# Sketched attention and four dense branches: a rearranged end, one more block in three products, and working tiles that begin at multiples of 64 bytes

## The chip, the cores and the metric

The kernel runs on one core of one Trainium2 chip, in one launch. The metric is the device time of that core in microseconds (us), the median of several executions. A separate execution was recorded by the hardware profiler; all the profile lines come from that one.

## The reference

Polynomial-sketch attention feeds a sum of four two-layer branches, weighted by token. In short:

```python
# q, k, v: (4 batches, 4 heads, 1088 tokens, 32); S1, S2: (8, 32)
a, b = x @ S1.T, x @ S2.T                      # x is q or k
phi(x) = outer(a, b)                           # 64 features a token and head
kv, z = phi(k).T @ v, phi(k).sum(tokens)
attn = (phi(q) @ kv) / (phi(q) @ z + 1e-6)
x = attn, heads side by side                   # (4352 tokens, 128)
p = domain_probs / (domain_probs.sum(-1) + 1e-9)
out = sum over e of p[:, e] * (relu(x @ w1[e]) @ w2[e])   # w1: 128 x 1024, w2: 1024 x 128, e = 0..3
```

Everything is float32.

## The kernel before

**Chunks, units, steps.** The 4352 tokens are cut into chunks `CHUNKS`: 128, 448, seven of 480, and 416 (numbers m = 0 to 9). A chunk passes through the four branches e = 0 to 3 one after the other; a pair (m, e) is called a unit here. The hidden layer has 1024 features, that is eight blocks k = 0 to 7 of 128. A step is two blocks, so a unit is four steps or eight half-steps, and a chunk is `NQ` = 16 steps; step 16m + 4e opens unit (m, e). Features lie on the 128 partitions and tokens along the free axis.

**First layer.** From chunk 1 on, the product of tokens and first weights is made of three faster products (type `F32R`): the tokens are split into `xa`, `xb`, `xd` and the weights into `wa`, `wb`, `wd`. `first` issues `wa`·`xa` and `wb`·`xb`, ScalarE scales the sum in PSUM (L1144), and one half-step later `third` adds `wd`·`xd` (L1194).

**Second layer.** For most blocks the hidden values are split too: ScalarE makes `ha` (L1198), VectorE makes `hb` (L1170, in `lower`) and, for two blocks at a time, `hd` (L1173). The three products with `vab`, `vb`, `vd` are called a, b and d. Any other block is one plain float32 product, called x, of `hid` (L1208, a ReLU on ScalarE) and the unsplit weights `w_sb`. Which blocks of a unit take three products is told by three sets: six blocks by default, seven for units in `MORE_IN`, all eight for units in `ALL_IN`. The split weights of the seventh and eighth blocks are made by `more_weight_parts` at steps listed by hand, in tiles called `vm` that reuse the room of attention tiles (`fs`, `y`, `sr`, `kvz` and others).

**The order on TensorE** is written by hand. `DEAL`, `DEAL_MORE`, `DEAL_ALL` and `DEAL_END` give each product of a unit a half-step, counted from the unit's first, at which it becomes due (`to_due`, `behind`, `passed`); within a half-step they go in the order of the list. Products a and b add up in PSUM tile o0, d and x in tile o1. When the last a or b is issued, ScalarE evacuates o0 (L1277). When the last d or x is issued, `gather` adds o1, multiplies by the token's weight `gate` and adds to `total` (for most units on GpSimd, L1357 to L1366), and it loads the gates of a later unit from DRAM (`load_gates`, SyncE's queue).

**The end.** The last unit is (9, 3), with `DEAL_END`. Its block 7 is left for the end as an x (`x7`): VectorE takes the ReLU and multiplies by `gate` in one operation (L1204). `finish` adds o1 to the evacuated o0, multiplies by `gate` and adds `total`, in three slices: tokens 256 to 415 (multiply and add on GpSimd), 0 to 127, 128 to 255. `by_token` first multiplies x7's hidden values by the weights with tokens on the output's partitions (L1300), then adds the finished sum through a product with the identity `eye` (L1306), which turns it to the same form. Copies bring the result from PSUM to `rows` (L1311), and four DMAs store it (L1314), two from SyncE's queue and two from ScalarE's.

**Where tiles lie.** The pools are laid one after the other, and each tile takes a multiple of 32 bytes of a partition. Up to `dsum` the sizes add up so that the next tile, `x_first`, begins 32 bytes past a multiple of 64. So do the tiles behind it in the pool `const` (`ring`, which holds the tokens, `wa`, `wb`, `wd`, and the four `vb`), and all tiles of the pools `loads` and `attn` but one. `rc`, the last one of `attn`, takes 96 bytes for its 20 numbers, and the pool `moe` behind it (`xa`, `xb`, `xd`, `ha`, `hb`, `hd`, `hid`, `gate`, `ev`, `total`) begins at a multiple of 64. Of the weights, `vab`, `vd` and `w_sb` lie ahead of `dsum`, at multiples of 64.

Of the kernel before, what the change touches and what calls it, by code (L numbers as in the profile page):

```python
# [25 lines left out]
def kernel(  # L26
# [24 lines left out]
    nc = tc.nc  # L51

    P = 128
    HP = 64
    B, H, S, D = q.shape
    E, DM, F = w1.shape
# [8 lines left out]
    XW = 640  # L65
# [10 lines left out]
        a0=4, b0=4, a1=4, b1=4, a3=5, x2=5, d0=6, d1=6, a4=7, b3=7, a5=8, b4=8, b5=9, d3=9, d4=9,  # L76
# [4 lines left out]
        a0=4, b0=4, a1=4, b1=5, a2=5, a3=5, d0=6, d1=6, b2=6, a4=7, b3=7, a5=8, b4=8, d2=8, d3=8,  # L81
# [5 lines left out]
        b5=9, a6=9, a7=9, b6=10, b7=10, d4=10, d5=11, d6=11, d7=12,  # L87
    )
    DEAL_END = dict(
        a0=4, b0=4, a1=4, b1=5, a2=5, a3=5, d0=6, d1=6, b2=6, a4=7, b3=7, a5=8, b4=8, d2=9, d3=9,  # L90
        b5=9, x6=10, d4=10, d5=10, x7=11,
    )
    ALL_IN = {(7, 1), (7, 2), (8, 1), (8, 2), (9, 1), (9, 2)}
    UNITS = [[P, 448, 512], [576, 512], [576, 512], [576, 512]]

    SPLITS = [
# [280 lines left out]
    def parts(m):  # L377

        c, end, at = START[m], START[m] + CHUNKS[m], 0
        while c < end:  # L380
            n = min(end, (c // S + 1) * S) - c
            yield c // S, c % S, n, at
            c, at = c + n, at + n

    gate = {}

    def load_gates(m, experts, queue=nc.sync):
        for e in experts:
            gate[m, e] = mpool.tile([P, CW], F32, tag="gate", bufs=2, name="gate")
            for b, c, n, at in parts(m):  # L390
                queue.dma_start(gate[m, e][:, at : at + n], gates[b, e, c : c + n].partition_broadcast(P))

# [280 lines left out]
    def attend_inverse(nd, laid):  # L673

        tiles, banks = banks_of(laid)
        rc = apool.tile([P, XW // 32], F32, tag="rc", name="rc")
        for i, t0, t1 in banks:
            nc.vector.tensor_scalar(
                out=rc[:, H * t0 : H * t1],
                in0=_ap(nd[i], 0, P, D, [[D + 1, H * (t1 - t0)]]),  # L680
                scalar1=1e-6, scalar2=1.0, op0=ALU.add, op1=ALU.mult,
            )
        nc.vector.reciprocal(rc[:, 0 : H * tiles], rc[:, 0 : H * tiles])
        return rc
# [261 lines left out]
    def more_weight_parts(e, k=OTHER[0]):  # L946

        w = second_weight(e, k)
        if k != OTHER[0]:
            abd = apool.tile([P, 3 * P], F32R, tag="fs" if e == 2 else "y", name="vm")  # L950
            a, b, d = (abd[:, P * i : P * i + P] for i in range(3))
        elif e % 2 == 0:
            if "sr" not in more_home:
                more_home["sr"] = cpool.tile([P, 6 * P], F32R, tag="sr", name="vm")
            a, b, d = (more_home["sr"][:, P * i : P * i + P] for i in range(3 * (e // 2), 3 * (e // 2) + 3))
        else:
            ab = apool.tile([P, 2 * P], F32R, tag="kvz", bufs=2, name="vm")
# [231 lines left out]
    def third():  # L1189

        while begun:
            i, j, k, g, w, x = begun.pop(0)
            n = g.shape[-1]
            nc.tensor.matmul(g, w, x, start=False, stop=True, skip_group_check=True)  # L1194
            m, e = steps[i][0], steps[i][1] // NP
            if k in three_of(m, e) and not whole(m, e):
                (ha, hb, hc), both_of = three_tiles(k, n, three_of(m, e))
                nc.scalar.activation(ha, g, ACTF.Relu, scale=NEAR)  # L1198
# [60 lines left out]
    def passed(m, e, what, k, hd):  # L1259

        n, o = CHUNKS[m], 0 if what in "ab" else 1
        if what == "x" and at_end(m, e) and k == FB - 1:
            return by_token(m, e, k, hd)
        if (m, e) not in acc:
            acc[m, e] = [None, None]
        if acc[m, e][o] is None:
            acc[m, e][o] = psum(ps_o, f"o{o}")
        first_one = (m, e, o) not in begun_o
        begun_o.add((m, e, o))
        last = last_of(m, e, o) == what + str(k)  # L1270
        b = block_of(m, e, k)
        w, h = (second_weight(e, b), hd) if what == "x" else (w2_parts[e][b]["abd".index(what)], hd["abd".index(what)])
        nc.tensor.matmul(acc[m, e][o][:, 0:n], w, h, start=first_one, stop=last)  # L1273
        if last and o == 0:
            tag = "rest" if at_end(m, e) else "ev"
            evs[m, e] = mpool.tile([P, CW], F32, tag=tag, bufs=1, name=tag)
            nc.scalar.activation(evs[m, e][:, 0:n], acc[m, e][0][:, 0:n], ACTF.Copy, scale=1.0 + R12)  # L1277
        if last and o == 1:
            finish(m, e) if at_end(m, e) else close(m, e)

    def finish(m, e):

        n, o1, ev, g = CHUNKS[m], acc.pop((m, e))[1], evs.pop((m, e)), gate.pop((m, e))
        for x, eng in ((slice(2 * P, n), nc.gpsimd), (slice(0, P), nc.vector), (slice(P, 2 * P), nc.vector)):
            nc.vector.tensor_tensor(out=ev[:, x], in0=ev[:, x], in1=o1[:, x], op=ALU.add)
            eng.tensor_tensor(out=ev[:, x], in0=ev[:, x], in1=g[:, x], op=ALU.mult)
            eng.tensor_tensor(out=ev[:, x], in0=ev[:, x], in1=total[m][:, x], op=ALU.add)
        last_sum[0] = ev

    last_sum = [None]  # L1290
# [1 line left out]
    def by_token(m, e, k, hd):  # L1292

        n = CHUNKS[m]
        ((b, at, _, _),) = parts(m)
        rows = lpool.tile([P, 4 * P], F32, tag="kn", name="rows")
        y = [psum(ps_h, "h") for _ in range(3)]
        cols = [(c, min(P, n - c), y[min(c // P, 2)], max(c - 2 * P, 0)) for c in range(0, n, P)]
        for c, w, to, x in cols:
            nc.tensor.matmul(  # L1300
                to[0:w, x : x + P], hd[:, c : c + w], second_weight(e, block_of(m, e, k)),
                start=(x == 0), stop=False, skip_group_check=True,
            )
        for part, copy in ((cols[0:1], nc.scalar.copy), (cols[2:], nc.scalar.copy), (cols[1:2], nc.vector.tensor_copy)):
            for c, w, to, x in part:
                nc.tensor.matmul(  # L1306
                    to[0:w, x : x + P], last_sum[0][:, c : c + w], eye[0][:, :],
                    start=False, stop=True, skip_group_check=True,
                )
            for c, w, to, x in part:  # L1310
                copy(rows[0:w, c : c + P], to[0:w, x : x + P])  # L1311
        for g in range(4):
            t = len([c for c in cols if c[1] > 32 * g])
            (nc.scalar if g % 2 else nc.sync).dma_start(  # L1314
                bass.AP(out.tensor, out.offset + (b * S + at // 32 + g) * DM, [[G * DM, 32], [4 * DM, t], [1, DM]]),
                _ap(rows, 32 * g, 32, 0, [[P, t], [1, DM]]),
            )
# [218 lines left out]
```

## Time and profile before

| what | value |
|---|---|
| median of 3 executions | 445.34 us (444.56 to 445.58) |
| the profiled execution | 445.73 us, span of the recorded instructions 443.8 us |
| TensorE busy | 436.2 us, 98% of the span |
| VectorE, ScalarE, GpSimd busy | 391.7, 345.7, 169.4 us |
| granted TensorE clock, mean | 0.995 of full speed |
| chain that ended last | TensorE 94%, VectorE 3%, DMA 1% |

The span runs from the first recorded instruction to the last; the time of the execution is 1.9 us more. A group's row gives its source line, engine, operation, output and inputs by tile name, shape and count, and then: busy us, mean ns of one | idle us of the engine just before them, with what ended that idle time. "PEld" is TensorE's weight load, which overlaps its products. A row of the timeline gives start and duration in us.

### The profile page before, as it was taken

How to read it: one execution, taken by the hardware profiler on the slowest of the kernel's cores; microseconds unless marked ns; L12 is line 12 of the kernel's file. 1: busy time of each engine (PE TensorE's matmuls, PEld its weight loads, DVE VectorE, ACT ScalarE, POOL GpSimd, SP SyncE). 2: the span in 40 equal slices, each digit the busy share in tenths (PEclk: the TensorE clock that was granted, in tenths of full speed). 3: DMA queues.
4: the chain of work that ended last, by engine and by line, in shares of the span. 5: the costliest groups of instructions: out<-in, count | busy, mean ns of one | idle time of the engine just before them, and what ended most of it. 6: DMA issues, size and time to landing. Idle time of an engine off the chain costs nothing.

```text
span 443.8 us, 8131 instructions
## 1 busy us (share of the span) xinstructions
PE 436.2 (98%) x2768; PEld 359.9 (81%) x2768; DVE 391.7 (88%) x623; ACT 345.7 (78%) x725; POOL 169.4 (38%) x244
## 2 busy tenths in 40 slices
PE   8999999999999999999999999999999999999994
PEld 5887678888887888878887888787888888889993
DVE  5998969978999889988998899989999998998994
ACT  4478888858878688868884888687888988888881
POOL 6348623212142023213351344132333673564372
PEclk9999999999999999999999999999999999999997
DMA  7956375225502331235104621251320112002100
GB/s 224 285 139 168 84 172 117 76 51 123 154 24 45 112 102 24 73 78 149 24 23 61 152 25 44 46 147 38 69 46 22 23 33 57 2 24 44 36 20 21
DMA packets 45561, 35.02 MB, mean 79 GB/s; under 512 B 21744, under 2 KB 40304, under 8 KB 45520
## 3 DMA queue, kind: packets, MB, share of 16 engines
q1 hardware_dynamic: 43952, 33.28, 30.3%
q0 software_dynamic: 1184, 1.05, 1.0%
q8 instruction: 22, 0.36, 0.3%
q10 hardware_dynamic: 384, 0.17, 0.2%
q14 instruction: 19, 0.16, 0.1%
HBM read 29.27 MB, written 5.21 MB: 78 GB/s over the span
## 4 chain that ended last, share of the span: by engine, by line
PE 94%; DVE 3%; DMA 1%; issue 1%; ACT 0%; SPq 0%; DVEq 0%; ACTq 0%
PE o L1273 41%; PE h L1194 14%; PE h L1142 14%; PE h L1143 14%; PE h L273 6%; PE o L1252 3%; PE h L460 1%; DMA kn<-in_k_dram 1%; PE o L273 1%; DVE qp L588 1%; PE h L1306 0%; DVE qa L870 0%; DVE rd L620 0%; DVE kp L482 0%; DVE qf L860 0%
## 5 line engine op out<-in xcount | busy, mean ns | idle before, releaser
L1144 ACT ACTIVATE h<-h 128x480 f32<-128x480 f32 (+2 forms) x288 | 158.9, 552 | 63.4 <-PE h L1143 56.2
L1170 DVE SCALAR_TENSOR_TENSOR hb<-h,ha 128x480 fp32r<-128x480 f32 (+2 forms) x229 | 142.6, 638 | 22.2 <-ACT ha L1198 20.7
L1173 DVE SCALAR_TENSOR_TENSOR hd<-ha,hb 128x960 fp32r<-128x960 f32 (+3 forms) x121 | 140.6, 1162 | 11.7 <-DVE hb L1170 0.5
L1198 ACT ACTIVATE ha<-h 128x480 fp32r<-128x480 f32 (+2 forms) x229 | 128.6, 561 | 0.1
L1142 PE MATMUL h<-xa,wa 128*128 128x480 f32 (+2 forms) x288 | 128.0, 445 | 0.0
L1194 PE MATMUL h<-xd,wd 128*128 128x480 f32 (+2 forms) x288 | 108.7, 378 | 0.1
L1143 PE MATMUL h<-xb,wb 128*128 128x480 f32 (+2 forms) x288 | 108.1, 375 | 0.0
L1364 POOL TENSOR_TENSOR ev<-ev,gate 128x256 f32<-128x256 f32 (+3 forms) x52 | 46.3, 890 | 143.3 <-DVE ev L1351 135.7
L1273 PE MATMUL o<-ha,vab 128*128 128x480 f32 (+2 forms) x204 | 76.8, 377 | 0.0
L1142 PEld LDWEIGHTS h<-xa,wa 128*128 128x128 f32 x288 | 54.2, 188 | 17.2 <-issue 10.6
L1143 PEld LDWEIGHTS h<-xb,wb 128*128 128x128 f32 x288 | 54.2, 188 | 16.9 <-issue 10.9
L1273 PE MATMUL o<-hd,vd 128*128 128x480 f32 (+2 forms) x204 | 64.1, 380 | 0.0
L1194 PEld LDWEIGHTS h<-xd,wd 128*128 128x128 f32 x288 | 54.0, 188 | 9.2 <-ACT h L1144 0.8
L1366 POOL TENSOR_TENSOR total<-total,ev 128x256 f32<-128x256 f32 (+3 forms) x52 | 56.6, 1088 | 4.1
L1273 PE MATMUL o<-hb,vb 128*128 128x480 f32 (+2 forms) x136 | 51.2, 376 | 0.0
L1357 POOL TENSOR_TENSOR ev<-ev,rest 128x256 f32<-128x256 f32 (+2 forms) x24 | 19.4, 830 | 61.7 <-ACT rest L1354 61.7
L1273 PEld LDWEIGHTS o<-hd,vd 128*128 128x128 f32 x204 | 37.9, 188 | 6.1 <-issue 0.9
L1273 PEld LDWEIGHTS o<-ha,vab 128*128 128x128 f32 x204 | 38.3, 188 | 5.1
L1273 PE MATMUL o<-hid,w_sb 128*128 128x480 f32 (+2 forms) x84 | 40.2, 560 | 0.0
L1208 ACT ACTIVATE hid<-h 128x480 f32<-128x480 f32 (+2 forms) x58 | 32.5, 560 | 0.9 <-PE h L1194 0.8
L1364 POOL TENSOR_TENSOR total<-ev,gate 128x256 f32<-128x256 f32 (+3 forms) x18 | 15.7, 895 | 39.3 <-issue 23.9
L1273 PEld LDWEIGHTS o<-hb,vb 128*128 128x128 f32 x136 | 25.5, 188 | 4.0 <-DVE hb L1170 0.4
(167 smaller groups left out, 472.3 us busy)
## 6 DMA issues: line engine op xcount, KB each, us to landing
gate<-gates SPq DMA_DIRECT2D x16, 240.0 KB, 3.5
kn<-in_k_dram SPq DMA_DIRECT2D x4, 544.0 KB
vn<-in_v_dram SPq DMA_DIRECT2D x16, 128.0 KB, 6.7
qp<-qd SPq DMA_DIRECT2D x8, 256.0 KB
qp<-qd SPq DMA_DIRECT2D x6, 288.0 KB, 4.7
qb<-qd SPq DMA_DIRECT2D x6, 288.0 KB
qn<-in_q_dram SPq DMA_DIRECT2D x3, 544.0 KB
w_sb<-in_moe_w_dram SPq DMA_DIRECT2D x3, 512.0 KB
```

Source lines behind the costliest of these rows:

```text
L273: nc.tensor.matmul(out(s), weights(s), moving(s), **flags)
L1142: nc.tensor.matmul(g, wa[:, e, w], xa, start=True, stop=False)
L1143: nc.tensor.matmul(g, wb[:, e, w], xb, start=False, stop=True)
L1144: nc.scalar.activation(g, g, ACTF.Copy, scale=1.0 + R12)
L1170: nc.vector.scalar_tensor_tensor(out=hb, in0=g, scalar=0.0, in1=high, op0=ALU.max, op1=ALU.subtract)
L1173: nc.vector.scalar_tensor_tensor(out=d2, in0=a2.bitcast(F32), scalar=R12, in1=b2.bitcast(F32), op0=ALU.mult, op1=ALU.subtract)
L1194: nc.tensor.matmul(g, w, x, start=False, stop=True, skip_group_check=True)
L1198: nc.scalar.activation(ha, g, ACTF.Relu, scale=NEAR)
L1208: nc.scalar.activation(hid[i][j], g, ACTF.Relu)
L1273: nc.tensor.matmul(acc[m, e][o][:, 0:n], w, h, start=first_one, stop=last)
L1364: nc.gpsimd.tensor_tensor(out=to[:, x], in0=ev[:, x], in1=g[:, x], op=ALU.mult)
L1366: nc.gpsimd.tensor_tensor(out=total[m][:, x], in0=total[m][:, x], in1=ev[:, x], op=ALU.add)
```

## The change

- One number tile more in the pool `const`: `by_row`, 16 bytes a partition, laid between `dsum` and `x_first`. `rc` gets 8 numbers more. Because of these two, the tiles from `x_first` to `rc` move by 32 bytes and those of `moe` by 64: all the tiles named above as lying 32 bytes off now begin at multiples of 64 (the second buffer of `kvx`, the one exception above, goes the other way).
- `by_row` holds the gates of the last chunk's branch 3 with tokens on partitions (four numbers a partition). A DMA on SyncE's queue, right behind that unit's `gate`, fills it, number by number.
- Unit (8, 0) joins `ALL_IN`: its block 7 becomes three products. The weights for it are split at steps 119 and 121, in the room of the attention tile `qa`.
- `DEAL_END`: b5 moves ahead of d2 and d3 within the same half-step.
- At the end, x7's ReLU goes from VectorE to ScalarE, behind the evacuation of o0, without the gate. The gate is applied by ScalarE after x7's product, in PSUM, with one number a partition from `by_row`. The evacuated o0 of tokens 0 to 255 is multiplied by the gate, and `total` added to it, ahead of o1's end (`near_end`). `finish` multiplies o1 by the gate for tokens 0 to 255 in one piece and adds it; then come tokens 256 to 415, now all on VectorE. The first two groups of tokens share one PSUM tile and one copy.

```diff
     DEAL_END = dict(
-        a0=4, b0=4, a1=4, b1=5, a2=5, a3=5, d0=6, d1=6, b2=6, a4=7, b3=7, a5=8, b4=8, d2=9, d3=9,
-        b5=9, x6=10, d4=10, d5=10, x7=11,
+        a0=4, b0=4, a1=4, b1=5, a2=5, a3=5, d0=6, d1=6, b2=6, a4=7, b3=7, a5=8, b4=8, b5=9,
+        d2=9, d3=9, x6=10, d4=10, d5=10, x7=11,
     )
-    ALL_IN = {(7, 1), (7, 2), (8, 1), (8, 2), (9, 1), (9, 2)}
+    ALL_IN = {(7, 1), (7, 2), (8, 0), (8, 1), (8, 2), (9, 1), (9, 2)}
...
     gate = {}
+    by_row = cpool.tile([P, 4], F32, name="by_row")
...
                 queue.dma_start(gate[m, e][:, at : at + n], gates[b, e, c : c + n].partition_broadcast(P))
+            if (m, e) == (NC - 1, E - 1):
+                ((b, c, n, at),) = parts(m)
+                queue.dma_start(by_row[:, :], gates[b, e, c : c + 4 * P].rearrange("(i p) -> p i", p=P))
...
-        rc = apool.tile([P, XW // 32], F32, tag="rc", name="rc")
+        rc = apool.tile([P, XW // 32 + 8], F32, tag="rc", name="rc")
...
-            abd = apool.tile([P, 3 * P], F32R, tag="fs" if e == 2 else "y", name="vm")
+            abd = apool.tile([P, 3 * P], F32R, tag={0: "qa", 1: "y", 2: "fs"}[e], name="vm")
...
                 if at_end(m, e) and k == FB - 1:
-                    nc.vector.scalar_tensor_tensor(
-                        out=hid[i][j], in0=g, scalar=0.0, in1=gate[m, e][:, 0:n], op0=ALU.max, op1=ALU.mult
-                    )
+                    last_block.append((hid[i][j], g))
                     continue
...
             nc.scalar.activation(evs[m, e][:, 0:n], acc[m, e][0][:, 0:n], ACTF.Copy, scale=1.0 + R12)
+            if at_end(m, e):
+                near_end(m, e)
...
+    def near_end(m, e):
+        n, ev, g = CHUNKS[m], evs[m, e], gate[m, e]
+        ((h, of),) = last_block
+        nc.scalar.activation(h, of, ACTF.Relu)
+        x = slice(0, 2 * P)
+        nc.vector.tensor_tensor(out=ev[:, x], in0=ev[:, x], in1=g[:, x], op=ALU.mult)
+        nc.vector.tensor_tensor(out=ev[:, x], in0=ev[:, x], in1=total[m][:, x], op=ALU.add)
     def finish(m, e):
-        for x, eng in ((slice(2 * P, n), nc.gpsimd), (slice(0, P), nc.vector), (slice(P, 2 * P), nc.vector)):
-            nc.vector.tensor_tensor(out=ev[:, x], in0=ev[:, x], in1=o1[:, x], op=ALU.add)
-            eng.tensor_tensor(out=ev[:, x], in0=ev[:, x], in1=g[:, x], op=ALU.mult)
-            eng.tensor_tensor(out=ev[:, x], in0=ev[:, x], in1=total[m][:, x], op=ALU.add)
+        x = slice(0, 2 * P)
+        nc.vector.tensor_tensor(out=t[:, x], in0=o1[:, x], in1=g[:, x], op=ALU.mult)
+        nc.vector.tensor_tensor(out=ev[:, x], in0=ev[:, x], in1=t[:, x], op=ALU.add)
+        x = slice(2 * P, n)
+        nc.vector.tensor_tensor(out=ev[:, x], in0=ev[:, x], in1=o1[:, x], op=ALU.add)
+        nc.vector.tensor_tensor(out=ev[:, x], in0=ev[:, x], in1=g[:, x], op=ALU.mult)
+        nc.vector.tensor_tensor(out=ev[:, x], in0=ev[:, x], in1=t[:, x], op=ALU.add)
...
     def by_token(m, e, k, hd):
...
-        for part, copy in ((cols[0:1], nc.scalar.copy), (cols[2:], nc.scalar.copy), (cols[1:2], nc.vector.tensor_copy)):
-            for c, w, to, x in part:
-                nc.tensor.matmul(
-                    to[0:w, x : x + P], last_sum[0][:, c : c + w], eye[0][:, :],
...
-            for c, w, to, x in part:
-                copy(rows[0:w, c : c + P], to[0:w, x : x + P])
...
+        pair = y[0]
+        y = [y[0][:, 0:P], y[0][:, P : 2 * P], y[1][:, 0:P], y[2][:, 0:P]]
+        for i, c, w in cols:
+            nc.tensor.matmul(
+                y[i][0:w], hd[:, c : c + w], second_weight(e, block_of(m, e, k)),
+                start=i != 1, stop=True, skip_group_check=True,
+            )
+        for i, c, w in cols:
+            nc.scalar.activation(y[i][0:w], y[i][0:w], ACTF.Copy, scale=by_row[0:w, i : i + 1])
+        for i, c, w in cols:
+            nc.tensor.matmul(
+                y[i][0:w], last_sum[0][:, c : c + w], eye[0][:, :], start=False, stop=True, skip_group_check=True
+            )
+            if i == 1:
+                nc.vector.tensor_copy(rows[:, 0 : 2 * P], pair[:, 0 : 2 * P])
+            elif i:
+                (nc.vector.tensor_copy if i == 2 else nc.scalar.copy)(rows[0:w, c : c + P], y[i][0:w])
...
-    for e, at in ((2, (113, 117)), (1, (114, 115))):
+    for e, at in ((2, (113, 117)), (1, (114, 115)), (0, (119, 121))):
```

More of the change, by code (lines that the diff above doesn't have):

```diff
@@ L1277, in passed @@
             nc.scalar.activation(evs[m, e][:, 0:n], acc[m, e][0][:, 0:n], ACTF.Copy, scale=1.0 + R12)
+            if at_end(m, e):
+                near_end(m, e)
         if last and o == 1:
             finish(m, e) if at_end(m, e) else close(m, e)
-    def finish(m, e):
-        n, o1, ev, g = CHUNKS[m], acc.pop((m, e))[1], evs.pop((m, e)), gate.pop((m, e))
-        for x, eng in ((slice(2 * P, n), nc.gpsimd), (slice(0, P), nc.vector), (slice(P, 2 * P), nc.vector)):
-            nc.vector.tensor_tensor(out=ev[:, x], in0=ev[:, x], in1=o1[:, x], op=ALU.add)
-            eng.tensor_tensor(out=ev[:, x], in0=ev[:, x], in1=g[:, x], op=ALU.mult)
-            eng.tensor_tensor(out=ev[:, x], in0=ev[:, x], in1=total[m][:, x], op=ALU.add)
+    last_block = []
+    def near_end(m, e):
[5 more added lines that the diff above has]
+        nc.vector.tensor_tensor(out=ev[:, x], in0=ev[:, x], in1=total[m][:, x], op=ALU.add)
+    def finish(m, e):
+        n, o1, ev, g, t = CHUNKS[m], acc.pop((m, e))[1], evs.pop((m, e)), gate.pop((m, e)), total.pop(m)
+        x = slice(0, 2 * P)
[5 more added lines that the diff above has]
+        nc.vector.tensor_tensor(out=ev[:, x], in0=ev[:, x], in1=t[:, x], op=ALU.add)
         last_sum[0] = ev
@@ L1297, in by_token @@
         y = [psum(ps_h, "h") for _ in range(3)]
-        cols = [(c, min(P, n - c), y[min(c // P, 2)], max(c - 2 * P, 0)) for c in range(0, n, P)]
-        for c, w, to, x in cols:
+        pair = y[0]
+        y = [y[0][:, 0:P], y[0][:, P : 2 * P], y[1][:, 0:P], y[2][:, 0:P]]
+        cols = [(i, c, min(P, n - c)) for i, c in enumerate(range(0, n, P))]
+        for i, c, w in cols:
             nc.tensor.matmul(
-                to[0:w, x : x + P], hd[:, c : c + w], second_weight(e, block_of(m, e, k)),
-                start=(x == 0), stop=False, skip_group_check=True,
-            )
-        for part, copy in ((cols[0:1], nc.scalar.copy), (cols[2:], nc.scalar.copy), (cols[1:2], nc.vector.tensor_copy)):
-            for c, w, to, x in part:
-                nc.tensor.matmul(
-                    to[0:w, x : x + P], last_sum[0][:, c : c + w], eye[0][:, :],
-                    start=False, stop=True, skip_group_check=True,
-                )
-            for c, w, to, x in part:
-                copy(rows[0:w, c : c + P], to[0:w, x : x + P])
+                y[i][0:w], hd[:, c : c + w], second_weight(e, block_of(m, e, k)),
+                start=i != 1, stop=True, skip_group_check=True,
+            )
+        for i, c, w in cols:
[8 more added lines that the diff above has]
+                (nc.vector.tensor_copy if i == 2 else nc.scalar.copy)(rows[0:w, c : c + P], y[i][0:w])
         for g in range(4):
-            t = len([c for c in cols if c[1] > 32 * g])
+            t = len([w for _, _, w in cols if w > 32 * g])
             (nc.scalar if g % 2 else nc.sync).dma_start(
```

## The prediction

> **What bounds the kernel now.** I read the page's busy times and chain first, then the time by stretches (one for each unit of chunk 8), then the groups, and last the timeline of the end.
>
> ```profile
> PE 436.2 (98%) x2768; PEld 359.9 (81%) x2768; DVE 391.7 (88%) x623; ACT 345.7 (78%) x725; POOL 169.4 (38%) x244
> PE 94%; DVE 3%; DMA 1%; issue 1%; ACT 0%; SPq 0%; DVEq 0%; ACTq 0%
> ```
>
> TensorE (PE) sets the time from about 28 us to 435 us. In that stretch an edit is worth what it takes from TensorE, or what it adds there by making it wait. Outside lie the start (VectorE and loads) and the last 8 us.
>
> ```profile
> 353.66:364.29 10.63, 10.63 (x49) 8.83 (x47) 9.58 (x13) 9.16 (x19) 7.71 (x11) 1.00 0.12 26
> 364.29:374.90 10.61, 10.61 (x48) 8.83 (x47) 9.20 (x13) 9.14 (x19) 5.36 (x6) 1.00 0.26 46
> 374.90:385.38 10.48, 10.48 (x49) 9.02 (x48) 9.81 (x13) 9.06 (x19) 2.98 (x3) 1.00 0.06 23
> ```
>
> These are units (8, 0), (8, 1), (8, 2), each from its first product to the next unit's: length, then busy us of PE, PEld, DVE, ACT, POOL. TensorE has no gap; VectorE (DVE) has about 1 us left in each. A unit's last products fall due in the next unit, so the plain float32 product x7 of (8, 0) runs in the second row, which is the longer for it.
>
> ```profile
> L1142 PEld LDWEIGHTS h<-xa,wa 128*128 128x128 f32 x288 | 54.2, 188 | 17.2 <-issue 10.6 <-PE h L460 0.2 <-DVE qT L575 0.2
> L1273 PEld LDWEIGHTS o<-ha,vab 128*128 128x128 f32 x204 | 38.3, 188 | 5.1
> L1273 PEld LDWEIGHTS o<-hb,vb 128*128 128x128 f32 x136 | 25.5, 188 | 4.0 <-DVE hb L1170 0.4
> L1170 DVE SCALAR_TENSOR_TENSOR hb<-h,ha 128x480 fp32r<-128x480 f32 x188 | 119.2, 648 | 17.2 <-ACT ha L1198 15.9 <-PE h L1143 0.9
> L898 DVE SCALAR_TENSOR_TENSOR xb<-xa,ring 128x480 fp32r<-128x480 f32 x7 | 4.5, 649 | 0.0
> ```
>
> `wa`, `vb` and `ring` lie 32 bytes off a multiple of 64; `vab`, `h`, `ha` do not. The rows make no difference between them.
>
> ```profile
> 433.41 1.34 POOL L1366 TENSOR_TENSOR total<-total,ev 128x160 f32<-128x160 f32 x1
> 433.89 0.35 PE L1273 MATMUL o<-hb,vb 128*128 128x416 f32 x1
> 434.28 0.52 ACT L1277 ACTIVATE rest<-o 128x416 f32<-128x416 f32 x1 [0.78 <-PE o L1273]
> ...
> 435.16 1.16 PE L1300 MATMUL h<-w_sb,hid 128*128 128x128 f32 x8
> 435.43 0.52 DVE L1285 TENSOR_TENSOR rest<-rest,o 128x160 f32<-128x160 f32 x2 [0.56 <-PE o L1273]
> 435.82 0.52 POOL L1286 TENSOR_TENSOR rest<-rest,gate 128x160 f32<-128x160 f32 x1 [1.07 <-DVE rest L1285]
> 435.98 0.52 DVE L1286 TENSOR_TENSOR rest<-rest,gate 128x128 f32<-128x128 f32 x1
> ...
> 437.65 0.29 DVE L1287 TENSOR_TENSOR rest<-rest,total 128x128 f32<-128x128 f32 x1
> ...
> 438.71 0.29 DVE L1311 COPY rows<-h 128x128 f32<-128x128 f32 x1 [0.77 <-PE h L1306]
> 439.08 0.81 SPq L1314 DMA_DIRECT2D out_dram<-rows  x2
> ```
>
> Once o1 is complete (435.43), VectorE works until 437.94 on seven operations of `finish`, two of them slowed from 0.29 to 0.52 and 0.50 us while GpSimd (POOL) works too. Then the last identity product (0.77) and copy (0.29), and the stores. Stores and closing take 443.8 - 439.08 = 4.7 us whatever comes before.
>
> **(8, 0) in three products.** Stretches whose TensorE work holds no x7 take 10.45, 10.50, 10.48 and 10.47 us ((7, 2), (7, 3), (8, 2), (8, 3)), mean 10.475; those with one take 10.61, 10.63 and 10.61, mean 10.617. The edit takes one away: **-0.14 us**, in (8, 1). Added on VectorE: one `hb` (0.65), `hd` for two blocks in place of one (1.24 against 0.74), two joins for the weights at 0.42 each at steps 119 and 121; on ScalarE two splits at 0.32 there. Those steps lie in (7, 1) and (7, 2), where VectorE is busy 9.91 of 10.61 and 9.85 of 10.45. The room of `qa` was read last at half-step 219, step 109. I cost this work at nothing: from the starts of products and the ends of the `hb` and `hd` before them, the least margin in (7, 1) to (8, 2) is 1.2 us, in (8, 3) 0.58. If that cover is gone, see the second rival.
>
> **64 bytes.** About 1000 weight loads move (288 each of `wa`, `wb`, `wd`, 136 of `vb`). From the starts of consecutive three-way products of 480 columns, the distance to a product with weights 32 off is 217.8 ns on average (703 of them) and to one with weights at a multiple of 64 also 217.8 (432). With a spread of some 2.6 ns the difference is known to 0.3 ns either way, so 1000 loads are worth -0.3 to +0.3 us; I take 0. The operands that stream (`xa`, `ha` and the like) lay at multiples of 64 before and still do. ScalarE's split takes 624 ns into `wa` and 631 into `vab`. Loads into attention tiles matter to the chain only at the start, where `kn` has 1%; -0.1 to +0.1 for that. [...]
>
> **The load of `by_row`.** It is issued behind `gate` of (9, 3), whose issue is at 426.17 for 0.35 us; behind it SyncE has only the stores at 439.08. Its 512 pieces of 4 bytes are not in this trace. The nearest rows: `out_dram<-ob`, 480 pieces of 128 bytes, issues in 0.5 us and lands in 2.7; the small `vn` pieces in the crowded start land in 8.0. I take 4, as for the `gate` loads (3.5 to 4.1): landed by 431. First use is at 435.8, below, so all of 2.7 to 8.0 is free. [...]
>
> **The end.** b5 takes d2's place, 433.50 for 433.89; its `hb` is complete at 433.24. TensorE's order behind it keeps its length. The evacuation moves to 433.89–434.41, and x7's ReLU (0.52) follows on ScalarE: 434.93, before L1300 at 435.16, which stays. Taking L1204 from VectorE frees 434.29–434.87. There `near_end` has two operations of 256 tokens at 0.414 (row L470), from 434.45. GpSimd is in L1366 until 434.75; I charge the first operation the 0.2 us that L1286 and L1287 paid, and `finish` starts at 435.52 (435.43 without). Two operations of 256 with gaps of 0.035: 436.38. Three of 160 (0.32 each, no GpSimd beside them): 437.46, against 437.94.
>
> Meanwhile ScalarE's four scalings (0.27 each by the copy L1311) can begin when the first pair of L1300 is through, 435.80; behind them ScalarE has only its copy and two stores, and the identity products wait for them. The first pair is scaled at 436.34, just ahead of 436.38; the others by 436.88, ahead of 437.46. The common copy of groups 0 and 1 fits on VectorE behind 437.46. Group 2's identity product and copy then take 0.77 and 0.29 as before (438.52), but group 3's product comes 0.34 behind group 2's, and its copy (0.25) ends at 438.82. The stores are issued at 438.88 instead of 439.08: **-0.20 us**. Bounds: -0.6 (no slowing by GpSimd, group 3 hidden) to +0.2 (the scalings or the smaller gaps cost as much again).
>
> **Sum.** 445.73 (span 443.8 and 1.9 around it) - 0.14 - 0.20 + 0 = 445.39 for a profiled execution. That one lay 0.39 above the median of the three, so on the median 445.34 - 0.34 = 445.0, that is -0.08%. A measurement of this kernel can tell about 0.2% (0.89 us) from no change; the three runs spread over 1.0 us. The terms' bounds give 444.3 to 445.6.
>
> **Rivals.**
>
> *Faster, 444.2.* Alignment is worth 0.3 us on weight loads and 0.1 at the start, and the end reaches its bound: -0.14 - 0.6 - 0.4 = -1.14. For it: the last chunk's stretches have no slack but TensorE's, so any nanosecond a product counts fully (1000 times). Against: equal means in the distances, and 188 ns in every row.
>
> *Slower, 446.3: VectorE falls behind in chunk 8.* In (8, 1) its work grows by 0.65 + 1.24, from 9.20 to 11.1 us in a stretch of 10.47: 0.6 late. (8, 2) can win back 10.48 - 9.81 = 0.67. If GpSimd slows VectorE further, as L1173's mean of 1235 ns against 1159 undisturbed shows, the delay reaches (8, 3), whose margin is 0.58, and TensorE waits. Against: (7, 3) and (8, 3) carry over 10.0 us without a wait. It turns the sign past -0.34 at a delay of 0.9 us there, and passes 0.2% at about 1.8, which gives 445.0 + 1.24 = 446.3.
>
> *Slower, 446.2: `by_row` is late.* It decides from a landing 9.3 us after issue (426.5 to 435.8) onward, about a microsecond for each further one; at 10.5 us the time is 446.2. Against: no load in the trace takes over 8.0.
>
> That the change doesn't do what it says (tiles still off) would alter nothing in the sum, as alignment has no term in it.
>
> **How the numbers follow.** The forecast has 0.60 (its own range 444.5 to 445.8, with some spread of the median), all of it within 0.2%. The faster rival has 0.23. VectorE late has 0.12, `by_row` late 0.05. The range for 8 times in 10 reaches to the faster rival and most of the way to the slower ones: 444.1 to 446.1.
>
> **What would show it.** Right: (8, 1) shrinks to 10.47 with no x7 in it; distances stay at 218 ns and weight loads at 188; `finish` ends about 0.5 us earlier relative to o1, ScalarE's copy is the last before the stores, 0.2 us earlier. Wrong: a wait of TensorE on `hb` or `hd` in (8, 1) to (8, 3); L1306 waiting for ScalarE or a load; distances that fall below 217.5 ns, which would give alignment its own term.

## The result and the profile after

The change makes the kernel faster by a little: 443.55 us (median of 22 executions, 442.73 to 445.08) against 444.86 (22, 444.20 to 445.67), ratio 0.9978, 95% interval 0.9970 to 0.9985. A second comparison, on another occasion, gave 443.48 against 444.76, ratio 0.9972 (0.9961 to 0.9984). The forecast was 445.0, no measurable change, with a range of 444.1 to 446.1; the time lies below it. A ratio here and below is that of a whole comparison, and it differs a little from the quotient of the two medians. The profiled execution of the changed kernel took 443.47 us, span 441.6.

The page after, busy times and chain:

```profile
PE 434.8 (98%) x2769; PEld 360.0 (82%) x2769; DVE 392.8 (89%) x626; ACT 346.8 (79%) x730; POOL 168.7 (38%) x242
...
PE 93%; DVE 4%; issue 1%; ACT 1%; DMA 0%; POOL 0%; DVEq 0%; ACTq 0%
```

TensorE still sets the time, with one instruction more and 1.4 us less work. A group of products and its weight loads, after (L1142 has become L1146), and the products' row before:

```profile
L1146 PEld LDWEIGHTS h<-xa,wa 128*128 128x128 f32 x288 | 54.2, 188 | 17.0 <-issue 10.4
...
L1146 PE MATMUL h<-xa,wa 128*128 128x480 f32 (+2 forms) x288 | 127.4, 442 | 0.0
```
```profile
L1142 PE MATMUL h<-xa,wa 128*128 128x480 f32 (+2 forms) x288 | 128.0, 445 | 0.0
```

The weight load is what it was, 188 ns. The product's mean was 445 ns and is 442: the busy times of consecutive products overlap (a three-way product of 480 columns starts 217.82 ns after the one before it, and 217.09 after the change), so this mean isn't the time that one costs. What counts is the distance from one start to the next, and that the stretches show. Chunks 1 to 8 in one stretch, from the first product of (1, 0) to the first of (9, 0), before:

```profile
28.30:395.85 367.55, 367.48 (x2056) 298.71 (x2055) 330.19 (x491) 296.39 (x609) 133.69 (x157) 1.00 0.30 72
```

and after, with the units (8, 0), (8, 1), (8, 2) below it:

```profile
28.03:394.64 366.61, 366.47 (x2056) 298.92 (x2055) 330.98 (x495) 296.37 (x611) 133.93 (x157) 1.00 0.30 72
```
```profile
352.79:363.38 10.59, 10.59 (x49) 8.85 (x47) 9.63 (x13) 9.14 (x19) 7.84 (x11) 1.00 0.08 26
363.38:373.80 10.42, 10.42 (x50) 9.00 (x48) 9.97 (x14) 9.03 (x19) 4.75 (x6) 1.00 0.20 47
373.80:384.21 10.41, 10.41 (x49) 9.03 (x48) 10.00 (x12) 9.05 (x19) 3.59 (x5) 1.00 0.08 25
```

(8, 1) lost its x7 (10.61 to 10.42). But (8, 0) and (8, 2), where the work is what it was, lost 0.04 and 0.07 too. So did 30 of the 35 units from (1, 0) to (9, 2). The mean distance from one three-way product of 480 columns to the next (from start to start, where the two follow each other directly) fell from 217.82 to 217.09 ns. About 1140 such distances at 0.73 ns are 0.83 us of the 0.94 us that chunks 1 to 8 lost. The granted clock was 0.995 and 0.996, and the kernels below at 0.999 (e1) and 1.000 (e3, e4, e12) have the longer distance, 217.78 to 218.14 ns, so it isn't the clock.

The end, timeline of the changed kernel:

```profile
432.54 0.52 ACT L1279 ACTIVATE rest<-o 128x416 f32<-128x416 f32 x1 [0.39 <-PE o L1275]
...
432.95 0.51 ACT L1291 ACTIVATE hid<-h 128x416 f32<-128x416 f32 x1
433.09 0.62 DVE L1293 TENSOR_TENSOR rest<-rest,gate 128x256 f32<-128x256 f32 x1
...
433.81 0.42 DVE L1294 TENSOR_TENSOR rest<-rest,total 128x256 f32<-128x256 f32 x1
434.34 0.42 DVE L1300 TENSOR_TENSOR total<-o,gate 128x256 f32<-128x256 f32 x1
434.43 1.19 ACT L1325 ACTIVATE h<-h,by_row 128x128 f32<-128x128 f32 x4 [0.97 <-PE h L1320]
...
435.92 0.33 DVE L1305 TENSOR_TENSOR rest<-rest,total 128x160 f32<-128x160 f32 x1
...
436.89 0.29 DVE L1333 COPY rows<-h 128x128 f32<-128x128 f32 x1 [0.31 <-PE h L1327]
437.23 0.26 ACT L1333 COPY rows<-h 32x128 f32<-32x128 f32 x1 [1.60 <-PE h L1327]
437.29 1.37 ACTq L1336 DMA_DIRECT2D out_dram<-rows  x2
437.51 1.16 SPq L1336 DMA_DIRECT2D out_dram<-rows  x2
```

`finish` takes 1.91 us from L1300 to the end of L1305, where the seven operations of before took 2.51. But it starts later, 0.39 us after the last o1 product for 0.12, because `near_end` works until 434.23; counted from that product, `finish` ends after 2.30 us for 2.63. ScalarE's copy is the last work before SyncE's stores.

### The profile page after: what moved, and what is told of

The parts are those of the page before. It is cut to its first block, busy times and chain, and to the rows that moved or that the text cites. A ratio compares the mean times of both kernels' runs of the same rounds, so it can differ in the third digit from the quotient of the medians.

```text
span 441.6 us, 8145 instructions
## 1 busy us (share of the span) xinstructions
PE 434.8 (98%) x2769; PEld 360.0 (82%) x2769; DVE 392.8 (89%) x626; ACT 346.8 (79%) x730; POOL 168.7 (38%) x242
## 4 chain that ended last, share of the span: by engine, by line
PE 93%; DVE 4%; issue 1%; ACT 1%; DMA 0%; POOL 0%; DVEq 0%; ACTq 0%
PE o L1275 40%; PE h L1198 14%; PE h L1146 14%; PE h L1147 14%; PE h L273 6%; PE o L1254 3%; PE h L464 1%; PE o L273 1%; DVE qp L592 1%; DMA s_raw<-in_S_dram 0%; DVE qa L874 0%; DVE hd L1177 0%; DVE hb L1174 0%; DVE rd L624 0%; DVE kp L486 0%
## 5 line engine op out<-in xcount | busy, mean ns | idle before, releaser
L1146 PE MATMUL h<-xa,wa 128*128 128x480 f32 (+2 forms) x288 | 127.4, 442 | 0.0
L1146 PEld LDWEIGHTS h<-xa,wa 128*128 128x128 f32 x288 | 54.2, 188 | 17.0 <-issue 10.4
L1379 POOL TENSOR_TENSOR ev<-ev,rest 128x256 f32<-128x256 f32 (+2 forms) x24 | 20.5, 877 | 61.1 <-ACT rest L1376 61.1
L1386 POOL TENSOR_TENSOR total<-ev,gate 128x256 f32<-128x256 f32 (+3 forms) x18 | 14.8, 842 | 39.3 <-issue 23.9
```

What stands on the lines that cost most here:

```text
L1146: nc.tensor.matmul(g, wa[:, e, w], xa, start=True, stop=False)
L1386: nc.gpsimd.tensor_tensor(out=to[:, x], in0=ev[:, x], in1=g[:, x], op=ALU.mult)
```

## The experiments

The table has what the profiles of all whole kernels show. W is the place of the first weights past a multiple of 128 bytes, V that of `vb` and the attention tiles, M that of the pool `moe`. "Distance" is the mean from start to start of three-way products of 480 columns. "1–8" is the stretch of chunks 1 to 8, "9" the one from there to the end of the last o1 product, "end" from there to the span's end. Times in us, distance in ns. Time and before are medians of the same comparison.

| kernel | W/V/M | distance | 1–8 | (8, 1) | 9 | end | time, before | ratio (95%) |
|---|---|---|---|---|---|---|---|---|
| before | 32/32/64 | 217.82 | 367.55 | 10.61 | 39.47 | 8.45 | | |
| the change | 64/64/0 | 217.09 | 366.61 | 10.42 | 39.31 | 7.63 | 443.55, 444.86 | 0.9978 (0.9970–0.9985) |
| e1 | 32/32/64 | 217.85 | 367.39 | 10.50 | 39.48 | 6.98 | 444.79, 444.56 | 1.0001 (0.9988–1.0015) |
| e2 | 64/64/0 | 217.05 | 366.72 | 10.58 | 39.33 | 7.18 | 443.58, 444.56 | 0.9981 (0.9962–1.0000) |
| e3 | 32/32/64 | 217.78 | 367.34 | 10.50 | 39.48 | 7.18 | 444.45, 444.56 | 0.9993 (0.9984–1.0001) |
| e4 | 32/32/64 | 217.81 | 367.54 | 10.61 | 39.46 | 7.00 | 444.51, 444.56 | 0.9998 (0.9986–1.0010) |
| e5 | 64/64/64 | 217.47 | 367.05 | 10.59 | 39.41 | 7.20 | 444.07, 444.34 | 0.9988 (0.9964–1.0013) |
| e6 | 32/32/0 | 218.09 | 367.73 | 10.60 | 39.40 | 8.63 | 445.19, 444.34 | 1.0015 (1.0004–1.0026) |
| e7 | 32/32/96 | 217.95 | 367.70 | 10.64 | 39.40 | 7.17 | 444.68, 444.34 | 1.0009 (0.9999–1.0019) |
| e8 | 0/0/0 | 217.52 | 366.99 | 10.46 | 39.38 | 8.76 | 443.77, 444.34 | 0.9990 (0.9980–1.0000) |
| e9 | 0/0/64 | 217.16 | 366.69 | 10.45 | 39.40 | 6.92 | 443.77, 444.54 | 0.9980 (0.9971–0.9988) |
| e10 | 64/96/0 | 216.96 | 366.61 | 10.57 | 39.32 | 7.17 | 443.32, 444.54 | 0.9981 (0.9971–0.9990) |
| e12 | 32/64/0 | 218.14 | 367.73 | 10.63 | 39.31 | 7.17 | 444.58, 444.54 | 1.0008 (0.9998–1.0018) |
| e14 | 64/96/0 | 216.97 | 366.44 | 10.43 | 39.30 | 6.98 | 443.59, 444.76 | 0.9974 (0.9963–0.9985) |
| e15 | 64/64/0 | 217.09 | 366.62 | 10.42 | 39.31 | 7.02 | 443.48, 444.76 | 0.9972 (0.9961–0.9984) |

The distance and the stretches repeat well: the change and e15 are one kernel and differ by 0.00 ns and 0.01 us, and the four profiles with the old places (before, e1, e3, e4) lie within 0.07 ns. That is what makes tenths of a nanosecond readable here.

**Which part carries it: e1 to e4.** e1 is the changed kernel with the tiles back in their old places:

```diff
-    by_row = cpool.tile([P, 4], F32, name="by_row")
+    by_row = {}
...
+                by_row[0] = mpool.tile([P, 4], F32, tag="by_row", bufs=1, name="by_row")
...
-        rc = apool.tile([P, XW // 32 + 8], F32, tag="rc", name="rc")
+        rc = apool.tile([P, XW // 32], F32, tag="rc", name="rc")
```

> The changed kernel with every tile where it lay before (by_row at the end of the pool moe, rc of 20 numbers). Theory A (the end carries the gain, alignment nothing): ratio to before 0.9978 as for the whole change (-1.0 us), distance between products the same as in the profile of after. Theory B (alignment takes about 0.7 ns from each three-way product, the end only the 0.2 us of the prediction): ratio 0.9993 (-0.3 us), mean distance of products of 480 columns back at 217.8 ns.

e2 is the kernel before with the tiles moved and nothing else (the uses of the longer `dsum` take its first `G` numbers):

```diff
-    dsum = cpool.tile([P, G], F32, name="dsum")
+    dsum = cpool.tile([P, G + 8], F32, name="dsum")
...
-        rc = apool.tile([P, XW // 32], F32, tag="rc", name="rc")
+        rc = apool.tile([P, XW // 32 + 8], F32, tag="rc", name="rc")
```

> The kernel before with 8 numbers more in dsum and in rc, so that all tiles lie as in the changed kernel; nothing else. Theory A: ratio 1.000, distance 217.8 ns. Theory B: ratio 0.9984 (-0.7 us), distance 217.1 ns, every unit 0.02 to 0.03 us shorter.

Chunks 1 to 8 of e1, then of e2:

```profile
29.00:396.38 367.38, 367.30 (x2056) 298.84 (x2055) 331.11 (x494) 296.44 (x611) 134.09 (x157) 1.00 0.30 72
```
```profile
28.38:395.10 366.72, 366.57 (x2055) 298.73 (x2054) 329.83 (x492) 296.27 (x609) 133.38 (x157) 1.00 0.29 72
```

Without the move, all the rest of the change is worth nothing that can be measured (1.0001); the move alone gives 0.9981 (its interval just reaches 1.0000; that of e10 below, 0.9971 to 0.9990, doesn't). It shortens chunks 1 to 8 by 0.83 us and chunk 9 by 0.14, with TensorE's counts and the loads' busy time (298.7) as they were.

e3 does only (8, 0) in three products (`ALL_IN`, the weights at steps 119 and 121, the room of `qa`), e4 only the new end (e1 without (8, 0)).

> The kernel before with unit (8, 0) in three products throughout; nothing else. Both theories: -0.14 to -0.19 us (ratio 0.9996 to 0.9997), unit (8, 1) 10.42 to 10.47 us, no wait of TensorE on hb or hd in (8, 1) to (8, 3). A rival, that VectorE falls behind: ratio over 1.000 and such waits.

> The kernel before with the new end alone: tiles where they lay before, (8, 0) as before. Theory A: ratio 0.9982 (-0.8 us); from the last o1 product's end to the span's end 7.6 us in place of 8.4. Theory B: ratio 0.9995 (-0.2 us), 8.2 us; the rest of the 0.8 in the profile of after was chance in the stores.

(8, 1) of e3:

```profile
363.87:374.37 10.50, 10.50 (x50) 9.01 (x48) 10.03 (x14) 9.07 (x19) 4.75 (x6) 1.00 0.22 47
```

10.611 to 10.498 is -0.11 us, a little less than expected, and TensorE is busy throughout. The end, from the last o1 product to the span's end, takes 7.00 in e4 and 7.18 in e3: -0.18. (Both theories had put e4's end higher, at 7.6 or 8.2, as they started from the 8.45 of the profile before; the last section tells why that one was long.) Both gains are below what the comparison of times can see (0.9993 and 0.9998, intervals across 1).

**Which tiles: e5 to e8, e10, e12.** e5 to e7 are the kernel before with other paddings (`dsum` + 8 and `rc` + 24 numbers; `rc` + 16; `rc` + 8); e8 is the changed kernel with `by_row` padded to 24 numbers and `rc` by 24.

> The kernel before with dsum 8 and rc 24 numbers longer: weights' parts, tokens, low parts and attention's tiles at multiples of 64, but the pool moe (the operands that stream through TensorE, and what the other engines make) at 64 past a multiple of 128 as before. Theory W (it is the place of the weights' parts): distance of products of 480 columns 217.1 ns, units of chunks 1 to 8 together 366.7 us, ratio 0.998. Theory M (it is the streamed operands, which moved from 64 past a multiple of 128 to a multiple of 128): 217.8 ns, 367.5 us, ratio 1.000.

> The kernel before with rc 16 numbers longer: the pool moe at multiples of 128, all else where it lay, 32 past a multiple of 64. Theory W: 217.8 ns, 367.5 us, ratio 1.000. Theory M: 217.1 ns, 366.7 us, ratio 0.998.

> The kernel before with rc 8 numbers longer: the pool moe 32 past a multiple of 64, all else where it lay. Theory W: 217.8 ns, ratio 1.000, as this pool's place does nothing. Theory M: more than 217.8 ns, for example 218.5 (the step from 128 to 64 taken once more), 368.3 us, ratio 1.002.

> The changed kernel with by_row 20 and rc 16 numbers longer still: weights' parts, tokens, low parts, attention's tiles and the pool moe all at multiples of 128. If a wider multiple for the weights brings more: distance under 217.1 ns, for example 216.4, and units of chunks 1 to 8 under 366.4 us. If 64 is enough for them: 217.1 ns, 366.6 us, ratio as for the change, 0.9978.

In e5 and e6 neither theory's numbers came out. Moving `moe` alone doesn't help (e6 is slower, 1.0015; e7 leans that way). Moving the weights from W = 32 to 64 shortens the distance at both places of `moe` that were tried, but by 0.35 ns at M = 64 (e5; its time, 0.9988, can't be told from 1) and by 1.0 at M = 0 (e2 against e6). And a rounder number isn't better: everything at multiples of 128 (e8) gives 217.52, less of the gain than the change's mixture. So neither place tells the distance by itself; the two act together.

e10 moves only the first weights (with `x_first` and `ring`), e12 only `vb` and the attention tiles; both move `moe` as the change does. In e10:

```diff
-    dsum = cpool.tile([P, G], F32, name="dsum")
+    dsum = cpool.tile([P, G + 8], F32, name="dsum")
...
-    wd = cpool.tile([P, E, F], F32R, name="wd")
+    wd_room = cpool.tile([P, E * F + 8], F32R, name="wd")
+    wd = wd_room[:, 0 : E * F].rearrange("p (e f) -> p e f", e=E)
```

(e12 has the longer `wd` and `rc` + 8.)

> The kernel before, with only x_first, ring, wa, wb and wd moved to multiples of 64 (dsum 32 bytes longer, wd 32 longer); vb, loads and attn stay 32 bytes off, moe moves by 64 as in the change. If the first weights carry the gain (864 of the 1000 loads moved), chunks 1 to 8 take 366.7 to 366.9 us for 367.5 and the time is 443.6 to 443.9. If vb or the attention tiles carry it, 367.4 to 367.6 and 444.4. If the gain goes by weight loads moved, 86% of 0.9: 366.8.

> The counterpart of e10_first_weights_only: the kernel before with only vb, loads and attn moved to multiples of 64 (wd 32 bytes longer, rc 32 longer); x_first, ring, wa, wb, wd stay 32 off, moe moves by 64. If the first weights carry the gain: 367.4 to 367.7 us for chunks 1 to 8 and 444.4. If vb or the attention tiles do: 366.7 and 443.6. By weight loads moved, 14% of 0.9: 367.4.

Chunks 1 to 8 of e10, then of e12:

```profile
28.08:394.68 366.60, 366.49 (x2055) 298.47 (x2054) 329.80 (x491) 296.19 (x609) 133.25 (x157) 1.00 0.30 72
```
```profile
28.03:395.76 367.73, 367.65 (x2056) 298.57 (x2054) 330.13 (x491) 296.26 (x609) 133.08 (x157) 1.00 0.31 72
```

With `moe` moved as in the change, the first weights (moved together with `x_first` and `ring`) carry the whole gain. `vb` and the attention tiles at a multiple of 64 bring none (e12); left off it they lose none (e10, 216.96 ns).

**Does it take the other engines: e11, e13.** e11 measures products by themselves.

> None of the reference's computation: 2304 products of type F32R with 480 columns, each with weights of its own, in groups of 48 that take 16 pairs of places: weights 0, 32, 64 or 96 bytes past a multiple of 128, streamed operand likewise. Two passes with TensorE alone, a third with VectorE and ScalarE working on operands of their own beside it; zeros are stored. If the weights' place costs TensorE time by itself, groups with weights at 32 or 96 show a larger mean distance by 1 to 2 ns than those at 0 or 64 in all passes, and the streamed operand's place nothing. If the cost comes from other engines at work, it shows in the third pass alone. If it is neither (a matter of this kernel's order), all 16 means agree within 0.2 ns in each pass.

One thing came out otherwise than that text has it. Nothing tied VectorE's and ScalarE's work to the third pass, so it ran beside the first (VectorE busy 160 of 169 us there); passes two and three had TensorE nearly alone. Means by group in ns, weights' place down, streamed operand's across, in the third pass:

| | 0 | 32 | 64 | 96 |
|---|---|---|---|---|
| 0 | 217.8 | 216.9 | 216.0 | 219.9 |
| 32 | 219.9 | 213.4 | 217.7 | 216.3 |
| 64 | 218.4 | 220.0 | 213.4 | 217.7 |
| 96 | 217.8 | 218.2 | 220.0 | 213.4 |

Groups of 48 with weights/stream at 0/64, 0/96 and 32/32, in the first pass, and the same three in the third:

```profile
35.49:45.86 10.37, 10.37 (x50) 9.01 (x48) 9.85 (x16) 9.83 (x18) 0.00 (x0) 1.00 0.01 2
45.86:56.42 10.56, 10.56 (x50) 8.98 (x49) 10.04 (x16) 9.99 (x19) 0.00 (x0) 1.00 0.00 0
66.97:77.22 10.25, 10.25 (x50) 8.98 (x48) 9.73 (x16) 9.71 (x18) 0.00 (x0) 1.00 0.00 0
```
```profile
369.57:379.94 10.37, 10.37 (x49) 9.01 (x48) 0.00 (x0) 0.00 (x0) 0.00 (x0) 1.00 0.00 0
379.94:390.50 10.56, 10.56 (x50) 9.01 (x48) 0.00 (x0) 0.00 (x0) 0.00 (x0) 1.00 0.00 0
401.05:411.30 10.25, 10.25 (x50) 8.98 (x49) 0.00 (x0) 0.00 (x0) 0.00 (x0) 1.00 0.00 0
```

The lengths are the same with VectorE and ScalarE at work (fourth and fifth numbers) and without. All three expectations of e11 fall. The distance goes neither by the weights' place alone nor by the other engines' work (on operands of their own), and it isn't constant: it goes by the pair, from 213.4 to 220.0 ns. In the first and third pass, equal places of 32, 64 or 96 are the fastest, and a stream 96 past the weights (0/96, 32/0, 64/32, 96/64) is the slowest. With equal lengths beside the other engines and without them, the means show that in this run the places of TensorE's own two reads, weights and stream, set the distance together.

The pair isn't all of it. The second pass went through the groups in reverse order, and some came out otherwise: 64/64 took 217.7 ns there and 213.4 in the other two, 32/32 took 220.1 and 213.4, 0/96 took 213.6 and 219.9. The first and third pass, which share one order, agree within 0.2 ns in the fifteen groups behind the first (the whole passes took 168.92 and 167.04 us), so it is the order that matters: a group also depends on how it was entered. Within a group the distances are regular. In 32/32 of the third pass they are 213 and 214 ns throughout, in the second pass 220; in 64/64 of the second pass they run through a cycle of about 218, 216 and 220.

e13 therefore replays the kernel's own order and places.

> None of the reference's computation: 120 three-way products of 480 columns in the order and with the places in memory that TensorE has in chunks 3 to 4 of the kernel before, without any other engine at work, for 18 layouts one after the other, and then once more in the reverse order of layouts: first weights, vb and attn W bytes past a multiple of 128 and moe M bytes past one, all 16 pairs of 0, 32, 64, 96, and the layouts of e10_first_weights_only and e12_rest_only. If TensorE's own reading of weights and streamed operands makes the difference, the mean distances follow those of the whole kernels: W/M 64/0 (the change), 0/64 and e10 at 217.0 to 217.2 ns, 64/64 and 0/0 at 217.5, 32/64 (before) at 217.8, 32/96 at 217.9, 32/0 and e12 at 218.1, each within 0.3. If it takes the other engines' accesses, all 18 agree within 0.3 ns.

| W/V/M | replay, two passes | whole kernel |
|---|---|---|
| 32/32/64 (before) | 217.54, 217.77 | 217.82 |
| 64/64/0 (the change) | 217.20, 217.47 | 217.09 |
| 64/96/0 (e10) | 216.73, 216.67 | 216.96 |
| 32/64/0 (e12) | 218.01, 218.04 | 218.14 |
| 32/32/0 (e6) | 218.30, 218.25 | 218.09 |
| 0/0/64 (e9) | 217.50, 217.34 | 217.16 |
| 32/32/96 (e7) | 217.59, 217.43 | 217.95 |
| 0/0/0 (e8) | 217.24 (second pass; in the first this layout opens the run) | 217.52 |
| 64/64/64 (e5) | 218.40, 218.61 | 217.47 |

Stretches of 120 products in the layouts of before, the change, e5, e10 and e12 (after the length: PE, PEld, DVE, POOL):

```profile
188.71:214.82 26.11, 26.11 (x122) 22.53 (x120) 0.00 (x0) 0.00 (x0) 1.00 0.00 0
240.93:266.99 26.06, 26.06 (x122) 22.52 (x120) 0.00 (x0) 0.00 (x0) 1.00 0.00 1
293.13:319.33 26.20, 26.20 (x121) 22.52 (x120) 0.00 (x0) 0.00 (x0) 1.00 0.00 1
450.24:476.25 26.01, 26.01 (x121) 22.52 (x120) 0.00 (x0) 0.00 (x0) 1.00 0.00 1
476.25:502.41 26.16, 26.16 (x121) 22.52 (x120) 0.00 (x0) 0.00 (x0) 1.00 0.00 1
```

With no other engine at work, all layouts from 216.7 to 218.8 ns appear, and e10 is the fastest, e6 and e12 among the slow ones, as in the whole kernels. The theory that all 18 agree falls. The other holds within 0.3 ns for seven of the nine, by the mean of the two passes (e8 by the second alone). It misses e7 by 0.4 (faster than before in the replay, slower in the kernel) and 64/64/64 by a full nanosecond (slow in the replay, middling in the kernel). Of the 0.73 ns between before and the change the replay gives 0.3. That isn't the choice of products: over the first 120 three-way products of chunk 3 and of chunk 4 the whole kernels have 217.6 and 218.0 (before), 216.3 and 216.9 (the change), 217.5 and 217.6 (e5). The replay leaves out the plain float32 products, all waits and the other engines; which of these makes the difference was not tried. So the replay shows that, with TensorE alone, the places it reads from made differences of this size; it doesn't show that they make all of the 0.73 ns in the kernel.

**Is there a better place: e9, e14, e15.** e9 is the changed kernel with `by_row` padded to 24 numbers.

> The changed kernel with by_row padded to 96 bytes: the tiles from x_first to rc begin at multiples of 128 (as in e8_all_at_128), those of moe 64 bytes past one. Theory A (the weights' place past a multiple of 64 counts, the streamed operand's does not): mean distance of three-way products 217.1 to 217.5 ns, chunks 1 to 8 in 366.6 to 367.0 us, time 443.5 to 443.8. Theory B (what counts is that weights and streamed operand do not begin at the same place of 128 bytes; vab and vd stay at multiples of 128): now all of them differ by 64, so the distance is the lowest yet, under 217.1, chunks 1 to 8 under 366.6 us, time under 443.3. Rival (place of the streamed operand alone, moe at 64 mod 128 is bad): distance back at 217.8, time 444.3.

217.16 ns and 366.69 us: the second theory (weights and stream 64 apart are best) wanted less than the change has and falls. The first theory's numbers fit here, but fail where the weights stay and only `moe` moves: e5 against e2, 217.47 and 217.05.

e14 is the changed kernel in the layout of e10, e15 the changed kernel itself beside it:

```diff
-        rc = apool.tile([P, XW // 32 + 8], F32, tag="rc", name="rc")
+        rc = apool.tile([P, XW // 32], F32, tag="rc", name="rc")
...
-    wd = cpool.tile([P, E, F], F32R, name="wd")
+    wd_room = cpool.tile([P, E * F + 8], F32R, name="wd")
+    wd = wd_room[:, 0 : E * F].rearrange("p (e f) -> p e f", e=E)
```

> The changed kernel with wd 32 bytes longer and rc 32 shorter: x_first, ring, wa, wb and wd at 64 past a multiple of 128 and moe at 0, as in the change; vb, loads and attn back at 32 past a multiple of 64 (96 past one of 128), as in e10_first_weights_only. If it is the pairs of places that count, not a multiple of 64, the distance is that of e10, 216.9 to 217.0 ns, chunks 1 to 8 take 366.4 to 366.6 us, and with the new end and (8, 0) in three products the time is 442.9 to 443.3, the shortest of all. If vb and the attention tiles want a multiple of 64, it falls behind the change by 0.1 to 0.2 us.

> The changed kernel once more, beside e14_first_at_64_rest_at_96 on the same chip: 443.3 to 443.7 us, distance 217.0 to 217.2 ns, chunks 1 to 8 in 366.5 to 366.7 us, as in its first profile. Its stores show whether the late landing of the first profile comes back.

In the profile e14 is the shortest of all, 366.44 against 366.62 for chunks 1 to 8. In time they are the same (443.59 and 443.48), and the 442.9 to 443.3 that was expected of e14 did not come: 0.2 us is below what the comparison sees. What it does show is that `vb` and the attention tiles need no multiple of 64.

## Why the prediction was wrong, point by point

- **The alignment term failed.** It had 0, with bounds of 0.3 us either way; e2 measured -0.97 (chunks 1 to 8 -0.83, chunk 9 -0.14). It is the whole of the measurable gain. The step behind it compared, inside the one trace of before, products with weights 32 off and products with weights at 64: 217.8 and 217.8 ns. That comparison could not carry the conclusion. The three-way products follow one another without a gap, the distance hangs on the pair of stream and weights, and it depends on how a group was entered (e11). Both kinds stood in the same mixed sequence, so both could be late by about the same amount, and the trace of the change shows that they were: the distance to products of the moved `wa`, `wb`, `wd` and `vb` fell from 217.8 to 216.9 ns, and the distance to products of `vab` and `vd`, whose weights did not move, fell too, from 217.9 to 217.3. Equal rows in one layout said nothing on another layout. (Some of the 432 had weights in tiles `vm` of the attention pool, 32 off; without the 59 `vm` products the means are still 217.8 and 217.9.) The bound of 0.3 us was a bound on the means' scatter, not on this.
- **The starting point was high, by the chance of a small sample.** The forecast 445.0 is 445.34 - 0.34, and 445.34 was the median of three executions; over 22 it is 444.86. Of the 1.45 us between 445.0 and 443.55, that is 0.48 and the alignment term 0.97. The bounds, added up straight, give 444.2 to 445.8, where the sum has 444.3 to 445.6; that decided nothing.
- The sentence that the streamed operands lay at multiples of 64 before and still do was true and beside the point: they moved from 64 to 0 past a multiple of 128, and e5 against e2 shows that this was worth half of the gain with the weights at 64 (217.47 to 217.05 ns), while with the weights at 32 it cost 0.27 (before to e6).
- **(8, 0) in three products was right**: -0.14 forecast, -0.11 in e3, in (8, 1) as said. VectorE was busy 9.97 and 10.00 us in (8, 1) and (8, 2), not 11.1 in (8, 1) alone, and TensorE didn't wait. The 11.1 added 1.24 for the `hd` of two blocks without taking off the 0.74 of the one that it replaces; over (8, 0) to (8, 2) VectorE's busy time grew by 1.01 us. That rival falls.
- **The end was right in its total, in part by luck.** SyncE's first store is issued 3.56 us after the last o1 product for 3.76, the forecast -0.20; ScalarE's even at 3.34. `near_end` pays 0.62 for 0.42 in its first operation while GpSimd works, the 0.2 charged. But the gaps around its second operation are about 0.1 us each, where 0.035 was put down, so that `finish` ends 2.30 us after the last o1 product and not 2.15; and what follows it, up to the end of ScalarE's copy, takes 1.24 for 1.36. The two errors nearly cancel. From last o1 product to span's end it is -0.18 (7.18 to 7.00).
- **"Stores and closing take 4.7 us whatever comes before" was wrong.** In e3 they take 3.4 us: 7.18 less 3.76. The profile of before had a late landing in it, as the last section tells. The forecast took only differences from it, so this cost nothing.
- **`by_row` was free, as said**: the scalings (L1325) waited for TensorE's product (0.97 us), not for the load. They took 1.19 us for four, 0.30 each, where 0.27 was put down. That rival falls.
- The rival that was faster, 444.2, had the right term in it, the tiles' places, but the wrong sizes: 0.4 for places and 0.6 for the end, where it was 1.0 and 0.2. It had the cost in the weight loads, and their mean stayed at 188 ns.

The sum with measured terms: -0.97 - 0.11 - 0.18 = -1.26 us. The comparisons gave 444.86 × (1 - 0.9978) = 0.98 us (0.67 to 1.33) and 1.25 us (0.71 to 1.73).

## What to carry to other kernels

Where TensorE runs without gaps, as here, treat the addresses of weights and streamed operands as a parameter of the kernel: two paddings of 32 bytes moved this one by 0.2%, and an edit that changes a tile's size can do the same unmeant. Compare the mean distance of products between two layouts; two kinds of products inside one layout didn't show it here (217.8 and 217.8 ns before). No rule of the form "a multiple of 64" or "of 128" held here, so try a few paddings and read the stretch that TensorE fills: it repeats to about 0.1 us (chunks 1 to 8: 367.55 and 367.54 in before and e4, 366.61 and 366.62 in the change and e15), while the times of one kernel spread over 1.5 to 2.4 (444.20 to 445.67 before, 442.73 to 445.08 after).

## What the runs showed of the hardware

- Products of 480 columns with weights of their own take 213.3 to 220.1 ns by the pair of places and by what went before, with TensorE alone, at a granted clock of 1.00 and a weight load of about 188 ns (e11). Why equal places are fast, and why one pair can settle at two values, stays open.
- The stores at the end landed late in some profiles. In those of before, e6 and e8 a packet of 16,384 bytes on the queue of kind "instruction" starts 4.2 to 4.4 us after the last o1 product, beside the stores, and takes 1.3 to 1.6 us; the end then takes 8.45 to 8.76 us. In e2, e10 and e12 such a packet comes earlier (2.8 to 4.1 us; the first stores are issued at 3.76), in e5, e9, e14 and e15 it comes 8 us after it or later, in e1, e3, e4 and e7 there is none: 6.92 to 7.20. In the first profile of the change it begins at 3.4 and runs into the first store: 7.63. ScalarE's issues of the two stores, e4 and then before:

```profile
438.56 0.84 ACTq L1337 DMA_DIRECT2D out_dram<-rows  x2
```
```profile
439.08 2.37 ACTq L1314 DMA_DIRECT2D out_dram<-rows  x2
```

  That the packet delays the stores is an inference from their coming together in the profiles of before, e6, e8 and the change; it wasn't tried by itself.
